# Moving the small column arithmetic of a gated state-space and dense kernel from VectorE to GpSimd, with one weight strip moved to another queue and a third output buffer

## The chip, the cores and the metric

The kernel runs on one core of a Trainium2 chip. The time is the device time of one execution, in microseconds (us); each kernel was run several times, always next to runs of the kernel before on the same chip. A profile shows one execution. Its span is shorter than that execution's time by 1.8 us (217.78 us for a span of 216.0). The profile names the engines PE (TensorE, matrix products), PEld (its weight loads), DVE (VectorE), ACT (ScalarE), POOL (GpSimd) and SP (SyncE, which issues most transfers).

## The reference, cut to what matters

```python
x = A_x                                             # 1 x 2048 x 640, bf16
g = sigmoid((x * gate_w).sum(-1, keepdims=True))
# a: a diagonal complex recurrence of 640 states
Lam_bar = exp(dt * Lam); B_bar = ((Lam_bar - 1.0) / Lam)[:, None] * Bmat
for t in range(L):
    h = Lam_bar * h + Bu[:, t, :]                   # Bu = x @ B_bar.T
y = 2.0 * einsum("blp,dp->bld", hseq, Cmat).real + x * Dskip
# b: a dense layer with 1728 hidden units
b = gelu(x @ w1 + b1) @ w2 + b2
return g * y + (1 - g) * b
```

The 2048 tokens are worked in four chunks of 512, counted from 0 in the code. The text calls chunk 2 "the third chunk" and chunk 3 "the last". The 640 states lie in five groups (`ks`) of 128 partitions.

## The kernel before: the parts that matter here

A complex recurrence with a constant turning factor is turned into two real scans: VectorE multiplies the input with tables of cosines and sines (`f1`, `f2`), combines them (`f3`), runs the two scans (`f4`), and turns the result back (`f6` to `f8`). Between two chunks the last column of each scan has to be turned by the angle of 512 steps; that is the carry (`f5`).

```python
        def f4(ri):
            if ri == 0:
                s["g"] = work.tile([P, 2, CH], BF16, name="g")        # two buffers
            init = 0.0 if c == 0 else carry[:, ri, ks:ks + 1]
            nc.vector.tensor_tensor_scan(s["g"][:, ri, :], r_c[:, ks:ks + 1].to_broadcast([P, CH]),
                                         s["v"][:, ri, :], init, ALU.mult, ALU.add)
        def f5():
            nc.vector.tensor_copy(out=glast[:, :, ks:ks + 1], in_=s["g"][:, :, CH - 1:CH])
            if ks == KS - 1:
                ...                                                   # two products, a sum, a difference
        ...
        later(ready, 0.61, f1)
        ...
        later(0, 1.23, lambda: f4(0))
        later(0, 1.23, lambda: f4(1))
        if c < NCH - 1:
            later(0, 0.1 if ks < KS - 1 else 0.5, f5)
```

The order of VectorE's instructions is fixed when the program is built. `later` puts work in a waiting list with a cost in us, `dve_now` places something that TensorE needs soon, and an internal clock (`ck.dve`, advanced by those costs) decides how much of the list is let out ahead of it. The costs are thus part of the order.

What TensorE needs soon are the "seeds": VectorE writes x times Dskip into a PSUM bank, TensorE adds ten matmuls of `CT` times the states to it, VectorE scales the sum by the gate into the output tile `ot`, and SyncE stores that.

```python
    def seed(ti):
        for d0, d1 in cuts(ti):
            p = bank()
            dve_now(ck.pe, 0.45, lambda: nc.vector.tensor_tensor(out=p[:, 0:d1 - d0], in0=xn[c][:, a, d0:d1], in1=Dbc[:, d0:d1], op=ALU.mult))
    ...
    def fin_a(c, at={}):
        let_out(0, c)
        for a in range(TPC):
            ot = fwork.tile([P, D], BF16, name="ot", bufs=2)
            if a < TPC - 2:
                seed(ti + 2)
            ...                            # 2 x 10 matmuls, then ot = gate * bank + gb, then the store
```

## Time and profile before

| | before |
|---|---|
| runs before the prediction | 218.41, 216.76, 218.45 us |
| span of the profiled run | 216.0 us |
| TensorE busy | 208.9 us |
| VectorE busy | 188.4 us, 385 instructions |
| GpSimd busy | 5.3 us, 20 instructions |
| TensorE's longest wait after the start | 2.56 us, at 173.75 us |

The page divides the span into 40 slices of 5.4 us and gives for each slice the busy share in tenths (9 means 90% or more). These are TensorE, VectorE and GpSimd of the kernel before:

```profile
PE   8999999999999999999999999999999959999994
DVE  2589999999989999997999999599999999995153
POOL 7020000000000000000000000000000000000000
```

TensorE has one hole, the 5 in the 33rd slice. After the start VectorE has three weaker slices, the 12th, the 19th and the 26th, and the last four, when its work is nearly done. GpSimd has done its work after the third. Its column of zeros is what the change wants to use. The lines for TensorE's hole and for VectorE's waits are in the prediction below.

### The profile page before, as it was taken

The page shows a single profiled execution, that of the slowest core. Times are in us where ns is not written, and L with a number is a line of the kernel's source. Part 1 is how long each engine was busy: PE and PEld are TensorE (multiplying, and loading weights), DVE is VectorE, ACT ScalarE, POOL GpSimd, SP SyncE. Part 2 cuts the span into 40 slices and gives each one's busy share as a digit, 9 for nine tenths or more (in the row PEclk, how much of TensorE's full clock was granted, in tenths as well). Part 3 has the DMA queues.
Part 4 walks back from the last instruction along what each step waited for, and adds up shares of the span by engine and source line. Part 5 has one row for each costly group of instructions (what it writes and reads, how often), then busy time and mean ns, then how long its engine had stood idle before and what let it go on. Part 6 is the DMA issues. An engine that isn't in the chain of part 4 may idle for free.

```text
span 216.0 us, 3540 instructions
## 1 busy us (share of the span) xinstructions
PE 208.9 (97%) x1372; PEld 125.2 (58%) x1383; DVE 188.4 (87%) x385; ACT 101.1 (47%) x182; POOL 5.3 (2%) x20
## 2 busy tenths in 40 slices
PE   8999999999999999999999999999999959999994
PEld 5645444454577545774466776444467737676773
DVE  2589999999989999997999999599999999995153
ACT  3599856665948769005634200556682310404200
POOL 7020000000000000000000000000000000000000
PEclk9999999999999999999999999999999999999999
DMA  7999999996000000051000006100000000110012
GB/s 181 242 194 208 213 227 313 281 210 152 3 0 0 3 0 0 14 181 65 0 0 3 0 0 179 36 30 0 2 17 0 0 3 0 61 64 0 0 62 64
DMA packets 33313, 16.23 MB, mean 75 GB/s; under 512 B 24720, under 2 KB 33296, under 8 KB 33296
## 3 DMA queue, kind: packets, MB, share of 16 engines
q1 hardware_dynamic: 32560, 15.37, 29.6%
q10 hardware_dynamic: 576, 0.62, 0.9%
q8 instruction: 11, 0.18, 0.3%
q14 instruction: 6, 0.05, 0.1%
q0 software_dynamic: 160, 0.01, 0.1%
HBM read 7.48 MB, written 2.62 MB: 47 GB/s over the span
## 4 chain that ended last, share of the span: by engine, by line
DVE 69%; PE 19%; DMA 6%; issue 2%; ACT 1%; SPq 1%; DVEq 0%
DVE g L505 19%; PE bank L669 10%; DVE wa L486 10%; DVE wb L486 10%; PE bank L610 7%; DVE v L486 6%; DVE hs L486 6%; DMA out_dram<-ot 4%; DVE bank L584 3%; DVE ot L674 3%; PE bank L276 2%; DMA xn<-in_A_x_dram 2%; DVE CT_re L474 2%; DVE CT_im L474 2%; DVE g L434 1%
## 5 line engine op out<-in xcount | busy, mean ns | idle before, releaser
L610 PE MATMUL bank<-w_sb,gel 128*128 128x384 bf16 (+1 forms) x416 | 57.9, 299 | 0.0
L610 PEld LDWEIGHTS <-gel 128*128 128x128 bf16 x416 | 40.3, 98 | 17.0 <-issue 0.8
L554 ACT ACTIVATE bu<-bank 128x512 bf16<-128x512 f32 x40 | 23.6, 597 | 37.7 <-PE bank L551 37.6
L669 PEld LDWEIGHTS <-hs 128*128 128x128 bf16 x330 | 31.7, 98 | 14.5 <-issue 2.7
L281 ACT ACTIVATE gel<-bank,colB 128x512 bf16<-128x512 f32 x52 | 33.7, 695 | 10.0 <-PE bank L276 9.8
L505 DVE TENSOR_TENSOR_SCAN g<-r_c,carry,v 128x512 bf16<-128x512 f32 x30 | 37.2, 1269 | 0.0
L618 ACT ACTIVATE gb<-bank,gcol 128x384 f32<-128x384 f32 (+1 forms) x32 | 15.0, 526 | 31.2 <-PE bank L610 16.1
L669 PE MATMUL bank<-CT_re,hs 128*128 128x320 bf16 (+2 forms) x165 | 27.1, 295 | 2.6 <-DVE bank L584 2.6
L674 DVE SCALAR_TENSOR_TENSOR ot<-bank,gcol,gb 128x320 bf16<-128x320 f32 (+2 forms) x33 | 17.4, 531 | 13.2 <-PE bank L669 9.5
L276 PE MATMUL bank<-xT,w1a 128*128 128x512 bf16 (+2 forms) x158 | 27.1, 324 | 0.2
L669 PE MATMUL bank<-CT_im,hs 128*128 128x320 bf16 (+2 forms) x165 | 27.1, 295 | 0.0
L551 PE MATMUL bank<-xT,BT_im 128*128 128x512 bf16 x99 | 24.8, 379 | 0.1
L551 PE MATMUL bank<-xT,BT_re 128*128 128x512 bf16 x97 | 24.5, 379 | 0.2
L276 PEld LDWEIGHTS <-w1a 128*128 128x128 bf16 x162 | 14.0, 99 | 11.7
L276 PE MATMUL bank<-xT,w1b 128*128 128x512 bf16 x80 | 17.9, 379 | 0.0
L599 ACT ACTIVATE bank<-b2bc 128x384 f32<-128x384 bf16 (+1 forms) x24 | 11.7, 528 | 11.6 <-DVE ot L674 11.6
L551 PEld LDWEIGHTS <-BT_im 128*128 128x128 bf16 x100 | 9.8, 98 | 11.8
L551 PEld LDWEIGHTS <-BT_re 128*128 128x128 bf16 x100 | 9.6, 98 | 11.0
L486 DVE TENSOR_TENSOR v<-wa,wb 128x512 bf16<-128x512 bf16 x40 | 15.2, 421 | 0.6
L584 DVE TENSOR_TENSOR bank<-xn,Dbc 128x320 f32<-128x320 bf16 (+2 forms) x33 | 14.3, 481 | 1.0 <-ACT gb L618 0.9
L486 DVE TENSOR_TENSOR wa<-TCOS,g 128x1024 bf16<-128x1024 bf16 x20 | 13.7, 685 | 0.1
L486 DVE TENSOR_TENSOR wa<-TCOS,bu 128x1024 bf16<-128x1024 bf16 x20 | 13.6, 682 | 0.0
(114 smaller groups left out, 171.7 us busy)
## 6 DMA issues: line engine op xcount, KB each, us to landing
out_dram<-ot SPq DMA_DIRECT2D x15, 160.0 KB, 1.8
xn<-in_A_x_dram SPq DMA_DIRECT2D x6, 320.0 KB, 4.3
w_sb<-in_B_w_dram SPq DMA_DIRECT2D x2, 640.0 KB, 5.8
w_sb<-in_B_w_dram SPq DMA_DIRECT2D x1, 800.0 KB, 8.4
w1b<-in_B_w_dram SPq DMA_DIRECT2D x5, 128.0 KB, 3.5
w1a<-in_B_w_dram ACTq DMA_DIRECT2D x3, 192.0 KB, 3.0
w1a<-in_B_w_dram SPq DMA_DIRECT2D x2, 192.0 KB, 3.2
xn<-in_A_x_dram SPq DMA_DIRECT2D x2, 192.0 KB, 6.4
```

Source lines behind the costliest of these rows:

```text
L276: nc.tensor.matmul(p[:, t0:t1], lhsT=w, rhs=xT[c][:, kd, t0:t1], start=(kd == 0) if first is None else first, stop=(kd == last), skip_grou ...
L281: nc.scalar.activation(out=gel[c][:, kf, :], in_=p[:, :], func=ACT.Gelu_apprx_tanh, bias=b1_c[:, kf:kf + 1])
L486: nc.vector.tensor_tensor(out=o, in0=a, in1=b, op=op)
L505: nc.vector.tensor_tensor_scan(s["g"][:, ri, :], r_c[:, ks:ks + 1].to_broadcast([P, CH]), s["v"][:, ri, :], init, ALU.mult, ALU.add)
L551: nc.tensor.matmul(p[:], lhsT=BT[ks >= KSA][:, kd, (ks % KSA if ks < KSA else ks - KSA) * P:][:, 0:P], rhs=xT[c][:, kd, :], start=(kd == 0 ...
L554: nc.scalar.activation(out=bu[:, ri, :], in_=p[:], func=ACT.Identity)
L584: dve_now(ck.pe, 0.45, lambda: nc.vector.tensor_tensor(out=p[:, 0:d1 - d0], in0=xn[c][:, a, d0:d1], in1=Dbc[:, d0:d1], op=ALU.mult))
L599: nc.scalar.activation(out=v, in_=src, func=ACT.Identity)
L610: nc.tensor.matmul(p[:, col:col + d1 - d0], lhsT=gel[c][:, kf, a * P:(a + 1) * P], rhs=w2_sb[:, kf, d0:d1], start=False, stop=False, skip_ ...
L618: nc.scalar.activation(out=gbs[ti][:, d0:d1], in_=p[:, col:col + d1 - d0], func=ACT.Identity, scale=gcol[:, 1, ti:ti + 1])
L669: nc.tensor.matmul(p[:, 0:d1 - d0], lhsT=hs[c][:, j, lo:lo + P], rhs=CT[:, j % KS, d0:d1], start=False, stop=(j == 2 * KS - 1), skip_group ...
L674: nc.vector.scalar_tensor_tensor(out=ot[:, d0:d1], in0=p[:, 0:d1 - d0], scalar=gcol[:, 0, ti:ti + 1], in1=gbs[ti][:, d0:d1], op0=ALU.mult, ...
```

## The change

**Intent.** VectorE is late at the third chunk. So the arithmetic on five or ten columns at a time (the decay `r_c`, the factors by which the C matrix is scaled, the carries) goes to GpSimd. A third buffer for `ot` takes the wait for the store away. The third strip of the first weight (`w1a` 2) leaves the ScalarE queue and is issued behind the token tiles, so that those land sooner. The diff, cut to its core:

```diff
-    load_w1a(nc.scalar, 2)
     load_x0(nc.sync, 3, 4, 0, KA * P)
+    load_w1a(nc.sync, 2)
...
-    load_xn(1, 0, H)
-    load_xn(1, H, TPC)
+    for a in range(TPC):
+        load_xn(1, a, a + 1)
...                                       (chunks 2 and 3: one load in place of two)
-    nc.vector.tensor_scalar(out=nsH[:], in0=sH, scalar1=-1.0, scalar2=None, op0=ALU.mult)
+    nc.gpsimd.tensor_scalar(out=nsH[:], in0=sH, scalar1=-1.0, scalar2=None, op0=ALU.mult)
...                                       (the other decay columns likewise; one reciprocal of ten columns stays)
     def factors():
-        tt = lambda o, a, b, op: nc.vector.tensor_tensor(out=o, in0=a, in1=b, op=op)
+        tt = lambda o, a, b, op: nc.gpsimd.tensor_tensor(out=o, in0=a, in1=b, op=op)
...
         def f5():
-            nc.vector.tensor_copy(out=glast[:, :, ks:ks + 1], in_=s["g"][:, :, CH - 1:CH])
-            if ks == KS - 1:
...
+            for t, f in zip(m, (cL, sL)):
+                nc.gpsimd.tensor_scalar(out=t[:], in0=g[:, :, CH - 1], scalar1=f[:, ks:ks + 1], scalar2=None, op0=ALU.mult)
+            for ri, op in ((0, ALU.subtract), (1, ALU.add)):
+                nc.gpsimd.tensor_tensor(out=carry[:, ri, ks:ks + 1], in0=m[0][:, ri:ri + 1], in1=m[1][:, 1 - ri:2 - ri], op=op)
...
-            later(0, 0.1 if ks < KS - 1 else 0.5, f5)
+            later(0, 0.0, f5)
...
-            if c == 0 and ks == 0:
-                later(0, 1.6, factors)
...
-            ot = fwork.tile([P, D], BF16, name="ot", bufs=2)
+            ot = fwork.tile([P, D], BF16, name="ot", bufs=3)
```

More of the change, by code (lines that the diff above doesn't have):

```diff
@@ L101 @@
     Dbc = const.tile([P, D], BF16, name="Dbc")
-    glast = const.tile([P, 2, KS], F32, name="glast")
     carry = const.tile([P, 2, KS], F32, name="carry")
@@ L269 @@
     thr = col("thr")
+    inv = col("inv", n=2 * KS)
+    q1 = col("q1")
+    q2 = col("q2")
     hs = [None] * NCH
@@ L392 @@
             nc.vector.tensor_copy(out=colB[:], in_=pA[:, 0:NB + KS])
-            nc.vector.tensor_tensor(out=dtl[:], in0=dt16[:], in1=lre_c, op=ALU.mult)
+            nc.gpsimd.tensor_tensor(out=dtl[:], in0=dt16[:], in1=lre_c, op=ALU.mult)
+            nc.gpsimd.tensor_tensor(out=q1[:], in0=lre_c, in1=lre_c, op=ALU.mult)
+            nc.gpsimd.tensor_tensor(out=q2[:], in0=lim_c, in1=lim_c, op=ALU.mult)
+            nc.gpsimd.tensor_tensor(out=inv[:, 0:KS], in0=q1[:], in1=q2[:], op=ALU.add)
         ff1_mm(banks[kf], 0, kf, 3, 0, CH, False, 3)
@@ L424 @@
     nsH = col("nsH")
-    rden = col("rden")
-    nc.vector.tensor_scalar(out=rden[:], in0=thr[:], scalar1=-1.0, scalar2=1.0, op0=ALU.mult, op1=ALU.add)
-    nc.vector.reciprocal(out=rden[:], in_=rden[:])
-    nc.vector.tensor_scalar(out=thr[:], in0=thr[:], scalar1=1.0, scalar2=None, op0=ALU.add)
-    nc.vector.tensor_tensor(out=r_c[:], in0=thr[:], in1=rden[:], op=ALU.mult)
-    nc.vector.tensor_scalar(out=nsH[:], in0=sH, scalar1=-1.0, scalar2=None, op0=ALU.mult)
+    nc.gpsimd.tensor_scalar(out=inv[:, KS:2 * KS], in0=thr[:], scalar1=-1.0, scalar2=1.0, op0=ALU.mult, op1=ALU.add)
+    nc.gpsimd.tensor_scalar(out=thr[:], in0=thr[:], scalar1=1.0, scalar2=None, op0=ALU.add)
+    nc.gpsimd.tensor_scalar(out=nsH[:], in0=sH, scalar1=-1.0, scalar2=None, op0=ALU.mult)
     for ks in range(KS):
@@ L436 @@
                                            scalar=cH[:, ks:ks + 1], in1=t[:], op0=ALU.mult, op1=ALU.add)
+    nc.vector.reciprocal(out=inv[:], in_=inv[:])
     nc.scalar.activation(out=TCOS[:, :, 0:HB], in_=FC, func=ACT.Identity)
@@ L444, in factors @@
     def factors():
-        tt = lambda o, a, b, op: nc.vector.tensor_tensor(out=o, in0=a, in1=b, op=op)
-        a_c = col("a_c"); b_c = col("b_c"); den = col("den"); q1 = col("q1"); q2 = col("q2")
+        tt = lambda o, a, b, op: nc.gpsimd.tensor_tensor(out=o, in0=a, in1=b, op=op)
+        a_c = col("a_c"); b_c = col("b_c")
+        den = inv[:, 0:KS]
+        tt(r_c[:], thr[:], inv[:, KS:2 * KS], ALU.mult)
         tt(a_c[:], r_c[:], cth, ALU.mult)
         tt(b_c[:], r_c[:], sth, ALU.mult)
-        nc.vector.tensor_scalar(out=a_c[:], in0=a_c[:], scalar1=-1.0, scalar2=None, op0=ALU.add)
-        tt(den[:], lre_c, lre_c, ALU.mult)
-        tt(q1[:], lim_c, lim_c, ALU.mult)
-        tt(den[:], den[:], q1[:], ALU.add)
-        nc.vector.reciprocal(out=den[:], in_=den[:])
-        nc.vector.tensor_scalar(out=den[:], in0=den[:], scalar1=2.0, scalar2=None, op0=ALU.mult)
+        nc.gpsimd.tensor_scalar(out=a_c[:], in0=a_c[:], scalar1=-1.0, scalar2=None, op0=ALU.add)
+        nc.gpsimd.tensor_scalar(out=den, in0=den, scalar1=2.0, scalar2=None, op0=ALU.mult)
         tt(q1[:], a_c[:], lre_c, ALU.mult)
@@ L457, in factors @@
         tt(q1[:], q1[:], q2[:], ALU.add)
-        tt(c2re[:], q1[:], den[:], ALU.mult)
+        tt(c2re[:], q1[:], den, ALU.mult)
         tt(q1[:], a_c[:], lim_c, ALU.mult)
@@ L461, in factors @@
         tt(q1[:], q1[:], q2[:], ALU.subtract)
-        tt(n2im[:], q1[:], den[:], ALU.mult)
-        nc.vector.tensor_scalar(out=n2re[:], in0=c2re[:], scalar1=-1.0, scalar2=None, op0=ALU.mult)
+        tt(n2im[:], q1[:], den, ALU.mult)
+        nc.gpsimd.tensor_scalar(out=n2re[:], in0=c2re[:], scalar1=-1.0, scalar2=None, op0=ALU.mult)
+    factors()
     def fold(ks):
@@ L508, in f5 @@
         def f5():
-            nc.vector.tensor_copy(out=glast[:, :, ks:ks + 1], in_=s["g"][:, :, CH - 1:CH])
-            if ks == KS - 1:
-                e1 = work.tile([P, 2, KS], F32, name="e1")
-                e2 = work.tile([P, 2, KS], F32, name="e2")
-                both = lambda t: t.rearrange("p (o k) -> p o k", o=1).to_broadcast([P, 2, KS])
-                tt(e1[:], glast[:], both(cL), ALU.mult)
-                tt(e2[:], glast[:], both(sL), ALU.mult)
-                tt(carry[:, 0, :], e1[:, 0, :], e2[:, 1, :], ALU.subtract)
-                tt(carry[:, 1, :], e1[:, 1, :], e2[:, 0, :], ALU.add)
+            g = s["g"]
+            m = [work.tile([P, 2], F32, name=n) for n in ("e1", "e2")]
+            for t, f in zip(m, (cL, sL)):
+                nc.gpsimd.tensor_scalar(out=t[:], in0=g[:, :, CH - 1], scalar1=f[:, ks:ks + 1], scalar2=None, op0=ALU.mult)
+            for ri, op in ((0, ALU.subtract), (1, ALU.add)):
+                nc.gpsimd.tensor_tensor(out=carry[:, ri, ks:ks + 1], in0=m[0][:, ri:ri + 1], in1=m[1][:, 1 - ri:2 - ri], op=op)
         def f6():
@@ L698 @@
     fin_a(0)
-    load_xn(2, 0, H)
-    load_xn(2, H, TPC)
+    load_xn(2)
     ssm(2, {KS - 1: lambda: first_banks(1)})
@@ L703 @@
     fin_a(1)
-    load_xn(3, 0, H)
-    load_xn(3, H, TPC)
+    load_xn(3)
     ssm(3)
```

## The prediction

> **What bounds the kernel now.** I read the page's busy shares first, then the waits, then TensorE's timeline around its longest wait, then the chain of waits, then VectorE's timeline.
>
> The page gives the first hint:
>
> ```profile
> span 216.0 us, 3540 instructions
> PE 208.9 (97%) x1372; PEld 125.2 (58%) x1383; DVE 188.4 (87%) x385; ACT 101.1 (47%) x182; POOL 5.3 (2%) x20
> DVE 69%; PE 19%; DMA 6%; issue 2%; ACT 1%; SPq 1%; DVEq 0%
> ```
>
> TensorE (PE) is busy 97% of the span, yet the chain that ended last runs for 69% over VectorE (DVE). Both can be true: VectorE paces the chain up to one point and TensorE is alone after it. The waits and TensorE's timeline show that point:
>
> ```profile
> PE bank L669 <- DVE bank L584: 2.6, 1, 2.6
> ...
> 166.51 7.24 PE L610 MATMUL bank<-w_sb,gel 128*128 128x384 bf16 x52
> 176.31 0.84 PE L669 MATMUL bank<-CT_re,hs 128*128 128x320 bf16 x5 [2.56 <-DVE bank L584]
> ```
>
> Line 669 needs a PSUM bank that VectorE has filled with x times Dskip (line 584, "seed"). The third chunk's first seed comes 2.56 us late. This is TensorE's one long wait after 6.3 us: everywhere else one group of matmuls begins where the last one ends (the five 512-column matmuls of line 551 start every 1.08 us from 97 to 107 us, 216 ns each). What TensorE has to do is therefore a floor, and the change takes no matmul away.
>
> Why VectorE is late shows in its own timeline. From 11.3 us to 176 us it has only three waits of half a microsecond or more:
>
> ```profile
> 65.21 0.89 DVE L474 SCALAR_TENSOR_TENSOR CT_re<-CT_re,c2re,ft 128x640 bf16<-128x640 bf16 x1 [0.96 <-ACT ft L470]
> ...
> 98.82 0.55 DVE L674 SCALAR_TENSOR_TENSOR ot<-bank,gcol,gb 128x320 bf16<-128x320 f32 x1 [1.26 <-DMA out_dram<-ot]
> ...
> 137.84 0.55 DVE L674 SCALAR_TENSOR_TENSOR ot<-bank,gcol,gb 128x320 bf16<-128x320 f32 x1 [2.33 <-PE bank L551]
> ```
>
> The second is the output buffer: `ot` has two, and the third tile waits for the first one's store. The last names TensorE, but I don't believe the name, since the matmuls of line 551 don't write that bank. The chain of waits has the true cause in the same place:
>
> ```profile
> 132.05 5.70 DMA out_dram<-ot
> 137.75 0.03 issue
> 137.77 0.02 DVEq L674
> 137.79 0.04 issue
> 137.84 0.55 DVE ot L674
> ```
>
> So 3.6 us of VectorE's waiting is the second output buffer: a store issued at 132.05, just behind the 640 KB load of the next tokens (issued at 130.53), lands only after 5.7 us.
>
> **What the Trainium skill says.** (1) "SBUF — State Buffer", section "SBUF: two separate sides": VectorE and GpSimd share one port pair as an exclusive lock, taken for a whole instruction; a VectorE instruction with two SBUF inputs counts against a GpSimd one that reads SBUF. Nearly all VectorE work here has two SBUF inputs. The trace agrees for GpSimd: its two casts of 3 and 2 columns last 0.76 and 0.80 us and each ends about 0.05 us after the 0.82 us VectorE instruction beside it. For VectorE it shows no cost: lines 413 and 414 start 0.74 us apart with a cast beside them (14.77, 15.51), and 416 and 417 start 0.74 us apart without (17.22, 17.96). (2) "Perfetto Trace Analysis", section "GPSIMD Engine Instruction": GpSimd spans are unreliable, go by start-to-start spacing; the two casts start 0.69 us apart, so I take 0.7 us for one small GpSimd instruction. (3) "Perfetto Trace Analysis", section "Optimizing Scalar/DVE Operations": because of the shared port, moving work from VectorE to GpSimd might not help. Only the two casts bear on that here. (4) "DMA: Bandwidth & Descriptors", section "Issuing engines are not separate DMA queues": all queues run on the same 16 engines. The trace agrees: one token tile of 64 KB issued at 2.12 us lands 4.1 us later, because the weight strips of the ScalarE queue (192 KB each) are moved at the same time.
>
> **The change part by part**, VectorE first; costs are start-to-start, since neighbours overlap.
> - Decay: five instructions on five columns run from 19.56 to 20.31 us, 0.75 us. All leave; one reciprocal of ten columns (about 0.1) comes in.
> - C-scale factors: seventeen instructions from 34.59 to 36.92 us, 2.33 us, leave. Also `dtl`, 0.1 us.
> - Carries: fifteen copies of the last column at 0.07 us each (32.52 to 32.59), 1.05 us; three times four more (60.94 to 61.38, then 111 and 153 us), 0.44 us each, 1.3 us. Sum 2.4 us.
> - Third output buffer: 1.26 + 2.33 = 3.6 us of waits.
> VectorE's total is 0.75 + 2.33 + 0.1 + 2.4 - 0.1 = 5.5 us of work and 3.6 us of waits, 9 us. Not all of it arrives at 175.8 us, because VectorE can't run ahead of matmuls whose results it reads. First 0.65 + 2.33 + 0.1 + 1.0 (first chunk's carries) + 0.14 = 4.2 us by 84 us, plus 1.26 makes 5.5; but the eight `ot` instructions of the first chunk end at 100.5 us and TensorE's last group there at 96.8, so 3.7 us stay. Then 0.8 for the second chunk's carries and 2.33 makes 6.8; the second chunk's last `ot` starts at 139.5 us and its matmuls end at 133.4, so 6.1 stay. Then two copies and the last five carry instructions (139.94, 146.49, 153.05 to 153.69) are 0.8. The late seed, at 175.77 before, is due at about 168.9, and TensorE is there at 173.75: **4.9 us of room**, so the whole 2.56 us wait should go and no more can be had from it.
>
> GpSimd gets 4 early instructions, 3 for the decay, 14 for the factors, 15 x 4 for the carries: 81, at 0.7 us some 57 us spread over 155 us. It must meet three times. `nsH`: the tanh ends at 17.2 us, then three instructions of 0.7 us end at 19.3, against VectorE's need at 19.56; a wait of up to 0.5 us is possible. `r_c`: the reciprocal at about 27.5, the product by 28.5, against the first scan near 29.5. The buffer `g`: the factors end at 28 + 14 x 0.7 = 38 us, the first carries at 41, against the third scan's reuse of that buffer at about 42. A scan's own carry is needed a chunk later, some 30 us, so no scan waits for it.
>
> Start: the last token tile lands at 6.24 us, and TensorE waits 0.4 us for it. Without 192 KB beside it, it should land about 0.6 us sooner (192 KB at the 310 GB/s of that stretch). But the load of `w1a` 2 takes 0.45 us of the SyncE queue, and the transposed tokens behind it land at 7.3 and 7.7 us against first uses near 7.8 and 8.4. The room there is about 0.5 us, so I keep 0.1 us of gain. The four loads of chunk 1's tokens and the single ones of chunks 2 and 3 are used long after landing; I count nothing.
>
> **Sum:** 216.0 - 2.56 - 0.1 = 213.3 us of span. A run's time is 1.8 us above its span (217.78 against 216.0). The three times before average 217.9 with a median of 218.4; less 2.7 they give 215.2 and 215.7. I take **215.5 us**.
>
> **The rivals.**
> - GpSimd's lock slows VectorE: if each of 81 instructions cost VectorE 0.1 us, that is 8 us, more than the work removed (the buffer's 3.6 us would still be gained), and part of the stall would stay: about 217 to 218. Against: the two casts that cost nothing. For: they are the only two.
> - A GpSimd result is late (`nsH`, or `g` at 42 us). VectorE would lose 0.5 to 3 us early on, and the caps above would swallow most of it by 100 us. The time stays near 215.5.
> - The output buffer alone does it: 3.6 us of waits is already more than 2.56. Same time, other cause; the moved work would then be hidden anyway.
> - The shifted transposes make TensorE wait at 7.8 us: up to 0.45 us more, 216.
> - The program places VectorE's instructions by an internal clock in which the removed work also shrinks, so scans move ahead of seeds and folds. An unlucky order could leave 1 us of wait.
>
> **Range and chances.** The floor is 216.0 - 2.56 - 0.4 = 213.0 of span, about 214.8 as a run; with the 0.8% spread of the times before I put the low end at 214.0. The high end, 217.2, has about half the stall kept. Faster by over 2% would need 4.4 us, more than the stall and the start hold together: 0.05. Slower by over 2% needs VectorE to lose about 12 us net against my sum: 0.03. Within 2%: 0.92.
>
> **What would show it.** In the changed kernel's timeline TensorE should have no wait over 0.3 us at the seeds of the third chunk, with the first seed near 169 us; no `ot` instruction should wait for a store; GpSimd instructions should last 0.4 to 1.2 us, as long as the VectorE instruction beside them; VectorE's busy time should be near 183 us. The step that would fail first is "GpSimd beside VectorE is free": then means of unchanged rows (the `wa` and `wb` products at 682 ns, the scans at 1,269) grow, or gaps open in front of them. The second is the start: the strips at 7.8 us.

## The result, and the profile after

| | before | after |
|---|---|---|
| median of six runs | 217.57 us (216.74 to 218.45) | 214.87 us (214.71 to 215.25) |
| span of the profiled run | 216.0 us | 212.9 us |
| TensorE busy | 208.9 us | 208.7 us |
| VectorE busy | 188.4 us | 183.5 us |
| GpSimd busy | 5.3 us | 62.7 us |

The ratio is 0.9876, with a 95% interval from 0.9842 to 0.9911: 1.2% faster. The ratios in this text are computed over fast runs alone, so they need not equal the ratio of the medians.

The page of the changed kernel begins with these lines; the last is the share of the engines in the chain of waits that ended last:

```profile
span 212.9 us, 3594 instructions
PE 208.7 (98%) x1372; PEld 125.2 (59%) x1383; DVE 183.5 (86%) x336; ACT 101.7 (48%) x182; POOL 62.7 (29%) x101
...
PE 97%; DMA 1%; issue 0%; DVE 0%
```

TensorE's busy time has not moved. What changed is the chain: 69% of it ran over VectorE before, now 97% runs over TensorE. VectorE no longer sets the end.

The timeline of TensorE at the third chunk (columns: start, duration, engine, line, operation, output<-inputs):

```profile
166.21 7.24 PE L608 MATMUL bank<-w_sb,gel 128*128 128x384 bf16 x52
173.29 0.84 PE L667 MATMUL bank<-CT_re,hs 128*128 128x320 bf16 x5
```

The bracket with the wait of 2.56 us is gone. Read against the two lines of before, the first group starts 0.30 us earlier and the second 3.02 us, so 2.72 us are won between the two: the wait of 2.56 us, and 0.16 us by which the next group now starts before the modelled end of the last. Laid side by side over the whole span, TensorE's two timelines differ by 0.15 us from the start on, by 0.06 and 0.08 us more from 83 and 122 us on, by these 2.72 us, and by 3.09 us in all.

VectorE at the same place:

```profile
167.69 2.45 DVE L508 TENSOR_TENSOR_SCAN g<-r_c,carry,v 128x512 bf16<-128x512 f32 x2
170.18 0.69 DVE L489 TENSOR_TENSOR wa<-TCOS,g 128x1024 bf16<-128x1024 bf16 x1
170.79 0.90 DVE L582 TENSOR_TENSOR bank<-xn,Dbc 128x320 f32<-128x320 bf16 x2
```

The seed starts at 170.79 us; it was 175.77 before. The prediction put it at 168.9. Ahead of it stand two scans that stood behind it before. The experiments come back to that.

The waits (columns: total us, times, longest us):

```profile
DVE ot L672 <- PE bank L667: 9.5, 7, 5.2
DVE bank L582 <- ACT gb L616: 7.1, 3, 6.0
...
POOL e L515 <- DVE g L508: 64.3, 13, 8.4
```

No `ot` instruction waits for a store any longer. The first line was there before (9.5 us: the end of the kernel, where TensorE works alone). The second was 0.9 us before and is harmless: VectorE, being ahead, now waits for ScalarE. GpSimd has 64 us of idle time between one carry and the next, so it is far from being a bound.

The groups of the page (columns: busy us, mean ns of one, idle time before, and its cause), first the scans of before, then two groups of after:

```profile
L505 DVE TENSOR_TENSOR_SCAN g<-r_c,carry,v 128x512 bf16<-128x512 f32 x30 | 37.2, 1269 | 0.0
```

```profile
L515 POOL TENSOR_SCALAR e<-g,cq 128x2 f32<-128x2 bf16 x15 | 18.3, 1222 | 64.3 <-DVE g L508 64.3
L508 DVE TENSOR_TENSOR_SCAN g<-r_c,carry,v 128x512 bf16<-128x512 f32 x30 | 37.2, 1271 | 0.0
```

The first product of a carry, on two columns, takes GpSimd 1.22 us, yet the scans of VectorE are as long as they were. Who waits for whom is seen in the two timelines around one carry of the changed kernel, GpSimd first, VectorE second:

```profile
44.58 1.35 POOL L515 TENSOR_SCALAR e<-g,cq 128x2 f32<-128x2 bf16 x1 [3.10 <-DVE g L508]
45.86 0.83 POOL L515 TENSOR_SCALAR e<-g,sq 128x2 f32<-128x2 bf16 x1
```

```profile
44.51 0.69 DVE L489 TENSOR_TENSOR wa<-TCOS,g 128x1024 bf16<-128x1024 bf16 x1
45.12 0.69 DVE L489 TENSOR_TENSOR wb<-TSIN,g 128x1024 bf16<-128x1024 bf16 x1
...
45.87 0.42 DVE L489 TENSOR_TENSOR hs<-wa,wb 128x512 bf16<-128x512 bf16 x1
46.20 0.42 DVE L489 TENSOR_TENSOR hs<-wb,wa 128x512 bf16<-128x512 bf16 x1
```

GpSimd's first product ends at 45.93 us, 0.12 us after VectorE's two products (45.81); its second ends at 46.69, 0.07 us after VectorE's pair (46.62). In these two cases GpSimd ends just after a VectorE instruction does; the longest product, 2.76 us from 76.16, ends at 78.92 behind four VectorE instructions on end, the last of which ends at 78.84. VectorE's own instructions follow each other at their usual spacing.

### The profile page after: what moved, and what is told of

It reads as the page before. It is cut to its first block, busy times and chain, and to the rows that moved or that the text cites. A ratio compares the mean times of both kernels' runs of the same rounds, so it can differ in the third digit from the quotient of the medians.

```text
span 212.9 us, 3594 instructions
## 1 busy us (share of the span) xinstructions
PE 208.7 (98%) x1372; PEld 125.2 (59%) x1383; DVE 183.5 (86%) x336; ACT 101.7 (48%) x182; POOL 62.7 (29%) x101
## 4 chain that ended last, share of the span: by engine, by line
PE 97%; DMA 1%; issue 0%; DVE 0%
PE bank L608 27%; PE bank L278 26%; PE bank L667 20%; PE bank L551 20%; DMA xn<-in_A_x_dram 1%; PE bank L624 1%; PE bank L304 1%; PE bank L240 0%; DVE ot L672 0%; PE bank L363 0%; PE bank L294 0%; PE bank L393 0%; PE bank L376 0%
## 5 line engine op out<-in xcount | busy, mean ns | idle before, releaser
L515 POOL TENSOR_SCALAR e<-g,cq 128x2 f32<-128x2 bf16 x15 | 18.3, 1222 | 64.3 <-DVE g L508 64.3
L508 DVE TENSOR_TENSOR_SCAN g<-r_c,carry,v 128x512 bf16<-128x512 f32 x30 | 37.2, 1271 | 0.0
L517 POOL TENSOR_TENSOR carry<-e,e 128x1 f32<-128x1 f32 x30 | 15.8, 547 | 1.3
```

The costliest lines, as they stand in the source:

```text
L515: nc.gpsimd.tensor_scalar(out=t[:], in0=g[:, :, CH - 1], scalar1=f[:, ks:ks + 1], scalar2=None, op0=ALU.mult)
L517: nc.gpsimd.tensor_tensor(out=carry[:, ri, ks:ks + 1], in0=m[0][:, ri:ri + 1], in1=m[1][:, 1 - ri:2 - ri], op=op)
```

## The experiments

The theory: the end is set by TensorE, whose only avoidable loss was the 2.56 us wait for the seed; any relief of VectorE larger than that removes it, and no more can be had. The rivals: the third buffer alone does it; the moved work alone does it; GpSimd beside VectorE costs something; the order by the internal clock eats part of the relief; the start gives a part of the gain. All kernels below gave correct results. Kernels of one group were run on one chip, and their runs of the kernel before are shared. One such run took 449 us, twice as long as any other, and is left out as a slow one.

To compare how much room VectorE has, I take TensorE's start of the third chunk's first `CT` matmul, less the 0.54 us that pass from the seed's start to that matmul in the kernel before (175.77 to 176.31), less the seed's start. For the changed kernel this is 173.29 - 0.54 - 170.79 = 1.96 us.

### The buffer alone, and the rest without it

`a_buf3` is the kernel before with one edit; `b_buf2` is the changed kernel with the opposite one:

```diff
-            ot = fwork.tile([P, D], BF16, name="ot", bufs=2)      # a_buf3
+            ot = fwork.tile([P, D], BF16, name="ot", bufs=3)
```

```diff
-            ot = fwork.tile([P, D], BF16, name="ot", bufs=3)      # b_buf2
+            ot = fwork.tile([P, D], BF16, name="ot", bufs=2)
```

> The kernel before with a third output buffer and nothing else. VectorE's order of instructions is unchanged. Theory (either half of the change is enough by itself): the two waits of ot for a store, 1.26 and 2.33 us, go, the third chunk's first seed moves from 175.8 to about 172.2 us, before TensorE gets there at 173.7, so TensorE's 2.56 us wait is gone: span about 213.3 us, ratio to before 0.988. Rival (the moved work is what counts, the buffer only moves VectorE's wait to another place): the seed stays within 1 us of 175.8 and the wait keeps more than 1.5 us, span 215 to 216, ratio 0.995 to 1.0.

> The changed kernel with two output buffers again: moved work alone, in the changed kernel's order, in which two more scans stand ahead of the third chunk's first seed than before. Theory: the two waits of ot for a store come back (1 to 2.5 us each), VectorE comes about 3.6 us later to that seed than the 170.8 us of the changed kernel, so at about 174.4 us, and TensorE, there at 173.3, waits 1 to 1.5 us: span about 214.2 us, ratio about 0.992. Rival (the moved work alone is enough in any order): no wait, span 212.9 to 213.1, ratio 0.988.

`a_buf3` took 215.17 us (214.69 to 215.76), ratio 0.9916 [0.988, 0.9951]. TensorE doesn't wait, no `ot` waits for a store, the seed starts at 172.78 us against TensorE at 174.23: 0.9 us of room. From VectorE's and TensorE's timelines:

```profile
172.78 0.90 DVE L584 TENSOR_TENSOR bank<-xn,Dbc 128x320 f32<-128x320 bf16 x2
```

```profile
174.23 0.84 PE L669 MATMUL bank<-CT_re,hs 128*128 128x320 bf16 x5
```

The expectation held, with both times 0.5 to 0.6 us later than named. Two of the four runs are 1 us longer than the others (spans of 213.8 and 213.9 against 212.8 and 212.9). The profile is of one of the long ones, and the loss is not at the seed: its first `w1b` matmul already starts at 12.36 us, against 11.70 in the kernel before.

`b_buf2` took 214.86 us (214.69 to 215.06), ratio 0.99 [0.9877, 0.9924]. I had expected a wait of 1 to 1.5 us for TensorE, and there was none: a miss. The lines of its waits and of VectorE's and TensorE's timelines at the seed show why:

```profile
DVE ot L672 <- DMA out_dram<-ot: 1.5, 2, 0.9
```

```profile
172.49 0.89 DVE L582 TENSOR_TENSOR bank<-xn,Dbc 128x320 f32<-128x320 bf16 x2
```

```profile
173.28 0.84 PE L667 MATMUL bank<-CT_re,hs 128*128 128x320 bf16 x5
```

The waits for stores are 1.5 us in this kernel, not the 3.6 that I had carried over from the profile of before. The seed comes 0.25 us ahead of need (TensorE starts at 173.28 us). So in these runs **either half alone was enough**, and the second one to be added had nothing left to remove.

The halves are not equally safe, though. The buffer takes 3.6 us of waits away, more than the 2.56 us. The other half brought the seed 3.28 us forward (from 175.77 us), and 2.1 us of that are the shorter waits for stores. That leaves about 1.2 us for the rest of this half, the moved work above all, in this order, an estimate by difference; the rooms with the third buffer give 1.05 (1.96 in the changed kernel, 0.91 in `a_buf3`). Both are less than the wait. With 3.6 us of waits for stores TensorE would, by the same estimate, have waited some 1.8 us in `b_buf2`. That the moved work alone is enough in this order is thus not shown.

### The order of VectorE's instructions

In the changed kernel 38 scans stand ahead of the third chunk's first seed, in the kernel before 36, since the costs of the removed work left the internal clock. `d_clock` is the changed kernel with the old costs put back, which restores the old order; `g_buf2_clock` is the same with two buffers.

```diff
-            later(0, 0.0, f5)
+            later(0, 0.1 if ks < KS - 1 else 0.5, f5)
...
             scan_ops(c, ks, bu, ck.act)
+            if c == 0 and ks == 0:
+                later(0, 1.6, lambda: None)
```

> The whole change, with the internal clock's costs of the kernel before, so the old order of scans, seeds and folds. My prediction assumed that order and gave 168.9 us for the third chunk's first seed; the changed kernel has it at 170.8. Theory (the 1.9 us are the two scans that the new order put ahead of the seed, not a cost of GpSimd): seed at 168.5 to 169.3 us, no wait of TensorE, span 212.9 to 213.2, ratio 0.988. Rival (GpSimd beside VectorE costs those 1.9 us): seed at 170.5 or later in the old order too.

> As the run before this one, but the costs in the program's internal clock are those of the kernel before, so that scans, seeds and folds stand in the order of the kernel before: moved work alone in the old order. Theory: VectorE gains 5.5 us of work less what it can't keep, about 3 to 4 us at the third chunk's first seed, which comes at 172 to 173 us, just before TensorE at 173.5: no wait or one under 0.3 us, span 213.0 to 213.3, ratio 0.988. Rival (order doesn't matter): the same span as the run before this one, whatever that is.

`d_clock` took 214.95 us (214.56 to 215.03), ratio 0.99 [0.9871, 0.993]. VectorE's timeline at the seed:

```profile
168.60 0.68 DVE L489 TENSOR_TENSOR wa<-TCOS,bu 128x1024 bf16<-128x1024 bf16 x1
169.20 0.89 DVE L584 TENSOR_TENSOR bank<-xn,Dbc 128x320 f32<-128x320 bf16 x2
```

The seed is back between the same neighbours as before (a `wa` product of `bu` ahead of it) and comes at 169.20 us, 0.3 us from the predicted 168.9. The room is 3.75 us rather than 1.96. So 1.8 us of room went to the order and not to GpSimd. `g_buf2_clock` took 214.95 us (214.73 to 215.55), ratio 0.9909 [0.9881, 0.9936]; its seed came at 169.62 us, earlier than the 172 to 173 that I had expected, in part since its waits for stores were only 1.4 us. Its room is 3.24 us (TensorE starts at 173.40); with the 3.6 us of waits of before, about 1.0 would be left, again an estimate. In the old order, then, the moved work should be enough without the buffer. Neither moves the time beyond its scatter: room that TensorE doesn't need is worth nothing.

### The smallest version, and the start

`f_buf3_w1a` is the kernel before with the third buffer and the moved strip, with nothing on GpSimd. `after_again` is the changed kernel, run beside it. `c_w1a` is the kernel before with the moved strip alone.

```diff
-    load_w1a(nc.scalar, 2)                                  # c_w1a, and in f_buf3_w1a with bufs=3
     load_x0(nc.sync, 3, 4, 0, KA * P)
+    load_w1a(nc.sync, 2)
```

> The kernel before with the third output buffer and the third weight strip behind the token loads; no work moved to GpSimd. Theory (the buffer alone takes TensorE's wait, the strip alone the scatter of the start): span 212.9 to 213.4 in every run, as the changed kernel, ratio within 0.2% of the changed kernel's beside it. Rival (the buffer-only kernel's two runs of 213.8 to 213.9 come from VectorE and not from the start): it again shows runs about 1 us longer.

> The changed kernel itself, as the measure for the three runs beside it on the same chip. Both theories: 214.9 us, span 212.9 to 213.3, ratio to before near 0.988.

> The kernel before with the third weight strip behind the token loads and nothing else. The spans of the kernel before scatter from 214.7 to 217.1 us, those of the changed kernel from 212.9 to 213.5. Theory: the scatter comes from the landing of the last token tile (3.6 to 4.8 us after its issue in old starts, 2.9 to 3.6 in new ones); with the strip moved TensorE's wait at the seed stays at 2.6 us and the spans lie within 0.6 us of each other, mean gain 0.1 to 0.6 us, ratio 0.997 to 0.9995. Rival (the start has nothing to do with the scatter): spans scatter over 2 us as before, ratio 1.0.

| | median us (lowest to highest) | ratio [95%] | spans |
|---|---|---|---|
| `after_again` | 215.03 (214.7 to 215.21) | 0.9896 [0.9839, 0.9952] | 212.8 to 213.4 |
| `f_buf3_w1a` | 215.09 (214.96 to 215.49) | 0.9904 [0.9856, 0.9953] | 213.2 to 213.6 |
| `c_w1a` | 217.17 (216.09 to 219.73) | 0.9994 [0.9946, 1.0041] | 214.3 to 217.8 |

The two-line version is as good as the whole change within what the runs can tell. Its seed comes at 172.10 us against TensorE at 173.56, 0.9 us of room, where the changed kernel has 2.0 us again (171.13 against 173.64). The moved strip alone gives nothing that can be seen in the time. I had expected its runs to agree better with each other, taking the start for the source of the scatter; they don't, so that expectation failed. Its waits:

```profile
DVE ot L674 <- DMA out_dram<-ot: 2.3, 2, 1.3
...
PE bank L669 <- DVE bank L584: 1.2, 1, 1.2
```

The waits for stores are 2.3 us here and TensorE's wait 1.2, where the kernel before had 3.6 and 2.56. Neither is a constant of the kernel.

`h_w1a4` was meant to beat both kernels: the changed kernel with one more strip issued earlier, from the ScalarE queue.

```diff
+    load_w1a(nc.scalar, 4)          # behind the first activation
...
-    load_w1a(nc.sync, 4)            # behind the transposed token loads
```

> The changed kernel with the fourth-used weight strip issued from ScalarE's queue after its first activation (near 3.7 us) instead of from SyncE's at 5.8 us; all later loads of SyncE's queue come 0.45 us sooner. In one run with an early last token tile TensorE waited for this strip until 8.9 us. Theory (the start is now bound by how soon the strips land): TensorE reaches the w1b matmuls at 11.2 to 11.4 us instead of 11.55 to 11.75, span about 0.2 us shorter, ratio 0.2% below the changed kernel's beside it. Rival (DMA engines are full from 2.5 to 9 us, so a strip that comes sooner makes the transposed tokens land later): no change, or up to 0.3 us longer.

It took 215.94 us (215.4 to 216.85), ratio 0.9946 [0.9904, 0.9988], about 0.5% slower than the changed kernel beside it (215.03). The matmuls with the second part of the weight (`w1b`) start at 12.39 us instead of 11.89. Next to `after_again`, the transposed token loads take 4.3 to 5.4 us to land instead of 3.4 to 4.2, and the strips of the SyncE queue 3.6 to 3.7 instead of 2.9 to 3.4: the strip that came sooner delayed the other transfers of that stretch, as the rival said, though the loss is larger than its 0.3 us. No version beat the changed kernel.

### GpSimd beside VectorE

`e_pool` adds sixty GpSimd products to the changed kernel, four per carry, with results that nobody reads:

```diff
+            for x in range(4):
+                d = work.tile([P, 2], F32, name="e3")
+                nc.gpsimd.tensor_scalar(out=d[:], in0=g[:, :, CH - 1], scalar1=(cL, sL)[x % 2][:, ks:ks + 1], scalar2=None, op0=ALU.mult)
```

> The changed kernel with four more products on GpSimd per carry, results thrown away: 60 more GpSimd instructions, nothing else changed. Theory (a GpSimd instruction waits for VectorE's, not the other way round, so its cost to VectorE is under 0.02 us): VectorE's rows keep their means (wa and wb 0.68 us, scans 1.27), the third chunk's first seed stays within 0.5 us of 170.8 to 171.1 us, TensorE doesn't wait, span 212.8 to 213.5. Rival (each costs VectorE 0.05 to 0.1 us): 45 of the 60 stand before that seed, so it comes 2.2 to 4.5 us later, and TensorE waits up to 2 us, span up to 215.

It took 214.86 us (214.66 to 215.25), ratio 0.9902 [0.9864, 0.9941]. From its page and its waits:

```profile
PE 208.4 (98%) x1372; PEld 124.8 (59%) x1383; DVE 183.9 (86%) x336; ACT 101.5 (48%) x182; POOL 115.9 (54%) x161
...
L508 DVE TENSOR_TENSOR_SCAN g<-r_c,carry,v 128x512 bf16<-128x512 f32 x30 | 37.2, 1270 | 0.0
```

```profile
DVE g L508 <- POOL e L518: 0.4, 2, 0.2
```

GpSimd is busy 53 us longer, VectorE 0.4 us longer, and the scans last 1270 ns. The seed comes at 171.65 us, 0.5 to 0.9 us later than in the two profiles of the changed kernel (171.13 and 170.79), a little more than the 0.5 us that I had allowed. Of that, 0.4 us are two real waits: a scan that reuses a `g` buffer waits until GpSimd has read it. The rest, at most 0.5 us over sixty instructions, is 0.01 us or less for each (all sixty end before that seed, by 155 us, and not 45 as the expectation has it). The rival that GpSimd slows VectorE by 0.1 us per instruction would have cost 6 us. It falls.

### How much room there is, and what a wait costs

`j_delay` puts four idle scans of 1.22 us, 4.9 us in all, on VectorE in the last chunk, ahead of the third chunk's seed. `before_look1` and `before_look2` are the kernel before, unchanged, each looked at once more.

```diff
+        if c == NCH - 1 and ks == 1:
+            def extra():
+                for _ in range(4):
+                    dmy = work.tile([P, CH], BF16, name="dmy", bufs=1)
+                    nc.vector.tensor_tensor_scan(dmy[:], r_c[:, ks:ks + 1].to_broadcast([P, CH]), s["v"][:, 0, :], 0.0, ALU.mult, ALU.add)
+            later(0, 0.0, extra)
```

> The changed kernel with four more scans on VectorE in the last chunk, results thrown away, some 4.8 us of work ahead of the third chunk's first seed. It measures the room. Theory: in the changed kernel the first half of that seed is done near 171.3 us and TensorE needs it at 173.3, room 2.0 us; with 4.8 us more TensorE waits 2.6 to 3.0 us, span 215.6 to 216.2, ratio to the kernel before about 1.0. Rival (the room is the 4.9 us of the prediction): no wait, span 213.

> The kernel before once more, for its profile. Two profiles show TensorE's wait at the seed 1.05 us shorter than the sum of ot's waits for stores (3.59 and 2.56; 2.3 and 1.25). Theory: this holds here too, and a look with longer store waits has the longer span, 213.0 plus the wait, give or take 0.5. Rival: the wait is not tied to the stores.

> As the look before: wait of TensorE at the seed = sum of ot's waits for stores less 1.05 us (within 0.2), span 213.0 plus that wait, give or take 0.5.

TensorE's timeline in `j_delay`:

```profile
176.32 1.30 PE L673 MATMUL bank<-CT_re,hs 128*128 128x320 bf16 x5 [2.58 <-DVE bank L588]
```

The 4.9 us brought back a wait of 2.58 us, as expected: the room was 2.3 us by this measure, 2.0 by the timelines. The time was not as expected: 219.53 us (217.93 to 219.81), ratio 1.0097 [1.0029, 1.0164], slower than the kernel before, though the wait is no longer than the one there. The line shows where it went on losing: the five matmuls take 1.30 us, where they took 0.84 in both kernels. Of its four runs three have a mean granted clock of 0.992 and spans of 217.6 to 218.0 us; the fourth has 0.999 and 216.1, inside the 215.6 to 216.2 that I had expected. In the profiled run the granted clock is 0.64 from 176 to 178 us and 0.51 from 178 to 180, which makes 3.4 us at half, from about 176.6 us on.

The same happened in one of the two looks at the kernel before. From VectorE's and TensorE's timelines in `before_look1`, then from its table of windows (columns: busy us and count of PE, PEld, DVE, ACT and POOL, granted clock, DMA share, GB/s):

```profile
99.16 0.55 DVE L674 SCALAR_TENSOR_TENSOR ot<-bank,gcol,gb 128x320 bf16<-128x320 f32 x1 [1.25 <-DMA out_dram<-ot]
...
138.20 0.55 DVE L674 SCALAR_TENSOR_TENSOR ot<-bank,gcol,gb 128x320 bf16<-128x320 f32 x1 [2.34 <-PE bank L551]
```

```profile
176.69 0.84 PE L669 MATMUL bank<-CT_re,hs 128*128 128x320 bf16 x5 [2.59 <-DVE bank L584]
...
178.22 1.54 PE L669 MATMUL bank<-CT_re,hs 128*128 128x320 bf16 x5
```

```profile
176.00:178.00 2.00, 1.31 (x10) 0.93 (x10) 1.97 (x5) 0.00 (x0) 0.00 (x0) 0.96 0.04 8
178.00:180.00 2.00, 2.00 (x9) 1.16 (x8) 2.00 (x5) 0.00 (x0) 0.00 (x0) 0.50 0.00 0
180.00:182.00 2.00, 2.00 (x12) 1.25 (x10) 2.00 (x5) 0.00 (x0) 0.00 (x0) 0.68 0.00 0
182.00:184.00 2.00, 2.00 (x17) 1.44 (x15) 2.00 (x6) 0.49 (x1) 0.00 (x0) 1.00 0.00 0
```

From 1.1 us after the end of the wait five matmuls take up to 1.54 us in place of 0.84, and the granted clock is half (0.50) from about 177.8 to 181.3 us: 0.96, 0.50 and 0.68 as means of 2 us each are 0.16 + 2.0 + 1.28 = 3.4 us of half clock. From the first `CT` matmul to the end it takes 218.0 - 176.69 = 41.3 us, against 216.0 - 176.31 = 39.7 in the profile of before; the clock cost 1.6 us. In that profile the same wait of 2.56 us was followed by a full clock in every window. A wait of that length thus halves the clock in some runs and not in others. What decides between them no run here settles. That the wait is needed for it fits all runs: of the 40 runs of the eight kernels that lack the wait in their profiles none has a mean clock under 0.998, while 10 of the 37 of the three kernels that have it (the runs next to the experiments and the two looks, the one of 449 us aside) are at 0.991 or 0.992.

`before_look2` had short waits, and its trace names the releaser that the prediction had to infer:

```profile
98.69 0.55 DVE L674 SCALAR_TENSOR_TENSOR ot<-bank,gcol,gb 128x320 bf16<-128x320 f32 x1 [0.80 <-DMA out_dram<-ot]
...
136.37 0.55 DVE L674 SCALAR_TENSOR_TENSOR ot<-bank,gcol,gb 128x320 bf16<-128x320 f32 x1 [0.99 <-DMA out_dram<-ot]
```

The same instruction for which two traces name matmuls of line 551 waits here for the store. It ran in 216.33 us with a span of 214.6, while `before_look1` had 219.77 and 218.0. Both looks kept the expected tie between the waits; both spans missed the expected ones, by 0.2 us here and by 1.9 us in `before_look1`, most of it the clock's. The four looks at the old order with two buffers line up:

| | waits for stores, us | TensorE's wait, us | span, us | clock |
|---|---|---|---|---|
| `before_look2` | 0.80 + 0.99 = 1.8 | 0.86 | 214.6 | 1.0 |
| `c_w1a` | 2.3 | 1.25 | 215.3 | 0.999 |
| before | 1.26 + 2.33 = 3.6 | 2.56 | 216.0 | 1.0 |
| `before_look1` | 1.25 + 2.34 = 3.6 | 2.59 | 218.0 | 0.992 |

TensorE's wait is the waits for stores less 0.9 to 1.0 us, every time. The store that the second wait is for, issued near 132 us behind two token loads, took 5.7 us to land in the two looks with the long wait and 4.4 us in the two others. So much of the scatter of the kernel before is that of its stores, passed on to TensorE; the start adds some tenths of a microsecond, as in `a_buf3`. Besides that, in 5 of its 25 runs beside the experiments (the one of 449 us aside) the mean clock was 0.991 or 0.992, with spans of 217.1 to 218.0 us; in the other 20 the spans were 214.3 to 216.3 with a mean of 215.3. (Two of the five count as slow runs and are in no ratio.) The ten runs of the changed kernel had 212.8 to 213.5, mean 213.1. Without the clock's part the change is therefore worth about 2.1 us on average.

## Why the prediction was right

- **TensorE's work is a floor, and the one long wait is what can be had.** Right. The wait is gone, the span was 212.9 us against 213.3 summed, the median 214.87 against 215.5. The sum plus 1.8 us would have given 215.1; the chosen 215.5 leaned on three runs of before whose median, 218.41, was high, and the kernel before has a wide scatter that is now explained.
- **The trace names the wrong releaser for the third wait of VectorE.** Right. `before_look2` names the store, and with a third buffer the wait is gone (`a_buf3`).
- **VectorE gives off 5.5 us of work.** Its busy time fell by 4.9 us to 183.5, where "near 183" was named; the prediction counted start to start, which includes gaps. GpSimd's 81 instructions took 62.7 - 5.3 = 57.4 us, against 57. Single ones were further apart than the 0.4 to 1.2 us foretold: 0.19 to 2.76 us, the long ones beside several VectorE instructions on end.
- **GpSimd beside VectorE is free.** Right for this size of instruction, by the scans at 1271 ns and by `e_pool`. The late `nsH` did not come about: it was ready at 16.3 us, since GpSimd worked it out ahead of the other two instructions.
- **4.9 us of room at the seed.** This is the step that was off, without harm, since 2.0 us were enough. The figure counted to the seed's start, while TensorE can begin 0.54 us later than that. The order moved by two scans, which took 1.8 us (`d_clock` against the changed kernel). The remaining 0.6 us are seen in `d_clock`: TensorE came at 173.49 us rather than 173.75, and the seed 0.3 us later than foretold. The prediction had the cause in its fifth rival, the internal clock, but the 4.9 us were computed as if the order stayed. With the order and the 0.54 us set right, the sum by chunks was good to 0.3 us.
- **3.6 us of waits for stores.** Taken as a constant, it is one draw: 1.8 to 3.6 us in four looks at the old order. This is why `b_buf2` went otherwise than I had expected. Whether the single larger token loads of the changed kernel shorten these waits (1.5 and 1.4 us in the two kernels that have both) or whether those were two more low draws stays open. (The load of 640 KB that the prediction names is two loads of 320 KB in the trace.)
- **The start, 0.1 us.** The profiles show 0.15 us, but the first `w1b` matmul starts anywhere from 11.70 to 12.36 us with the old order of loads and from 11.50 to 12.23 with the new one. The gain is not resolved, and `c_w1a` does not show it in the time.
- **The rival "the output buffer alone does it".** Also true: `a_buf3` has no wait, and `f_buf3_w1a` equals the whole change. Its opposite held in the runs of `b_buf2`, but with short waits for stores; the moved work alone, in the changed kernel's order, was worth 1.0 to 1.2 us by the estimates above, less than the wait.
- **Not foreseen.** After a wait of 2.6 us the clock may halve for 3.4 us. Removing the wait removes that too, which is one reason why the changed kernel's runs lie so close together; the other is that the scatter of the stores no longer reaches TensorE.

## What to carry to other kernels

When the bounding engine has a single hole, first ask what is the cheapest relief that covers it: here a third buffer, one number in the source, took the wait away as the whole change with its 81 moved instructions did, and what the two give doesn't add up. Look at the kernel more than once before taking a wait from its profile as a constant. And when an instruction order comes from modelled costs, removing work reorders what remains, so check the position of the critical instruction and not only how much time was freed ahead of it.

## What the Trainium skill lacked or had wrong

- "TensorE: Matmul & The Clock Gate", section "🔬 Part 1: The HAM clock gate (the "warmup" mystery)", gives half the clock after at least one idle window of about 3.4 us. Here waits of 2.58 and 2.59 us were followed by half the clock in two profiles, and one of 2.56 us in a third was not. A wait well under the stated length is thus not safe. The page calls the window free-running, which would suit a result that differs from run to run, but no run here tests that; the half clock set in 1.1 us after the matmuls went on in one profile and about 0.2 us after in the other. The 3.4 us that the half clock lasted agree with the time that the page gives for coming back.
- "SBUF — State Buffer", section "SBUF: two separate sides", has whichever engine comes second blocked for a whole instruction. That showed on one side only: GpSimd's first product of each carry was stretched to 1.22 us on average, while sixty more of them cost VectorE 0.01 us each or less, apart from 0.4 us of waits for a buffer. How unequal the two sides are, the page doesn't say.
- "Perfetto Trace Analysis", section "GPSIMD Engine Instruction": the spacing from start to start of two casts gave 0.7 us for an instruction, and 81 instructions averaged 0.71 us. The way of reading was good for the sum; single instructions ran from 0.19 to 2.76 us.
- None of the pages that I read has it that the named releaser of a wait can change between traces: the same `ot` instruction was put down to matmuls in two profiles (2.33 and 2.34 us) and to the store in two others (0.99 us each).
